# Attention values with tokens on partitions, turned by VectorE, in a fused attention and feed-forward kernel

## The chip, the cores and the metric

The kernel runs on one core of one Trainium2 chip. The metric is the device time of one execution in microseconds (us), as a median over several executions. A profile of one execution lies beside the times. Its engines are PE (TensorE's matmuls), PEld (TensorE's loads of the stationary operand), DVE (VectorE), ACT (ScalarE), POOL (GpSimd) and SP (the engine that issues the DMAs).

## The reference, cut to what matters

Chunked attention with eight memory tokens, then two dense layers with a gate between them, all in float32:

```python
B, H, S, D = 4, 8, 768, 64           # chunk, left_ctx, right_ctx, n_mem = 32, 16, 8, 8
for c in range(S // 32):
    k_full = concat([mem_k, k[:, :, c0 - 16 : c0 + 40]])        # 64 keys per chunk of 32 queries
    v_full = concat([mem_v, v[:, :, c0 - 16 : c0 + 40]])
    scores = (q_c @ k_full.T) / 8
    a = exp(scores - max); a = a / (sum(a) + 1e-9)
    out[:, :, c0 : c0 + 32] = a @ v_full
x = out.transpose(0, 2, 1, 3).reshape(3072, 512)
h = x @ w_in                                                    # 512 -> 2048
g = where(h >= 1, h, where(h <= -1, 0, (h + 1) ** 2 / 4))
return g @ w_out                                                # 2048 -> 512
```

## The kernel before, in words

The 3072 tokens are cut into six blocks of 512. Attention is done for half a block (256 tokens, eight chunks, four pairs of heads) at a time. The dense layers take one block in 16 steps; step s computes 128 of the 2048 hidden columns.

Float32 products of the dense layers are made from three terms: each operand is split into a high part (rounded to the type fp32r) and a low part (the rest), and high by high, low by high and high by low are added up. So x, the attention's output, is kept as `xth` and `xtl`, the gated hidden values as `gh` and `gl`, and the weights as two halves of one tile `wr`. Each x tile has the features of a pair of heads on its 128 partitions and the tokens along its free axis.

Attention of one half block goes through these stages:

- `pe_scores`: 64 small matmuls write scores into a pair of PSUM banks (`ps_s`, tag "s"). The loaded operand is 32 queries wide, the moving one 64 keys, the contraction is the 64 features of a head. The inner loop runs over the two heads, which lie in the two halves of the input partitions.
- `less_max`, an Exp on ScalarE and `normalise`: the softmax, in the tile `pr` with 32 queries of four chunks on the partitions.
- `transpose_prob`: six VectorE transposes of 32 by 32 squares, `pr` to `pt`. Two take all 128 partitions and four take 32 partitions each, since they change the partition group.
- `pe_values`: 64 small matmuls write into the same pair of banks (`ps_x`, tag "s" too). The loaded operand is the values `v` of one head, 64 features wide, and the moving one is `pt`, 32 queries; the output has features on 64 partitions. The half `a` of the input partitions is in the outer loop and the head `h`, which chooses the output partitions, in the inner one.
- `x_high` (ScalarE, two casts out of PSUM into `xth`) and `x_low` (VectorE, two subtractions into `xtl`).

Order is written out by hand, and every engine executes its own instructions in that order. The list `FIRST` orders everything up to the end of the second block: a name such as `n2` stands for the next stage of a half block (n0 to n3 are the halves of the second and third block), `J15` or `E9` for the next stage of a step of the first or second block, `w7` for a part of a weight's decoding, `+` for the next DMA of a list. From the third block on a loop over s sets the order. A step of it issues on TensorE the small matmuls that are due, then `pe_hidden(s)` (12 matmuls of 512 columns into `ps_h`), then `pe_out(s - 2)` (12 into `ps_o`). The gate's instructions for step s - 1 (`gate_sum`, `gate_high`, `gate_low`: writes `gw`, `gh`, `gl`) stand early in step s, and its three ScalarE activations for step s (`gating`) late. Half blocks of the next block begin at steps 3 and 9 (`STARTS`), with scores, softmax, transposes and values one step apart each.

Buffers: `ps_h` has two, `gh` and `gl` three, `gw` and `gt` two, `pr`, `pt`, `qk`, `v` and the "s" banks one, `xth` and `xtl` two.

Of the kernel before, what the change touches and what calls it, by code (L numbers as in the profile page):

```python
# [8 lines left out]
F32 = mybir.dt.float32  # L9
# [33 lines left out]
    w15 J13 J15 n1 J15 n1 J14 C0 J15 n1 J14 n1 n1 C0 n1 n1 J15 C1 n1 n1 J15 n1 C1 n1 n1 C1 C0 C1 C2  # L43
    J15 J15 C0 C1 n1 J15 J15 C0 C2 C2 C0 + n1 C2 n1 n1 C3 C2 C1 C3 C3 D0 C3 C3 C2 D0 D0 D1 D0 D0 n2
    D1 D1 D2 D1 + n2 C3 D1 D2 n2 D0 D2 n2 D2 D3 n2 D2 D1 n2 n2 D3 n2 E4 D3 n2 D3 n2 n2 n2 D2 E4 D3
    n2 E5 n2 E4 E4 E4 D3 E5 E6 E5 E5 E5 E4 E6 E6 E6 n2 E6 E7 + n2 n2 n2 n3 E7 E5 + n3 n3 E7 E8 n3 E7
    n3 n3 n3 E6 n3 E8 n3 n3 n3 E9 n3 n3 n3 E8 n3 E7 E8 E9 E8 E7 + n3 E9 E9 n3 n3 E9 E10 E8 E10 E10
    E10 E11 E10 E9 E11 E11 E11 E12 E11 E10 E12 E12 E12 E13 E12 E11 E13 E13 E13 E14 E13 E12 E14 E14
    E14 E15 E14 E13 E15 E15 E15 E15
"""  # L50

LAST = 2
# [16 lines left out]
def attn_ffn_kernel(ctx: ExitStack, tc: tile.TileContext, first_qk, first_v, qk, vw, w, out):  # L69
# [98 lines left out]
        yield  # L168


    scores_of, prob, prob_t, banks, xts, both = {}, {}, {}, {}, {}, {}

    def x_of(blk):
        if blk not in xts:
# [139 lines left out]
    def transpose_prob(key):  # L314


        src = prob.pop(key).rearrange("p g (s k) -> p g s k", s=2)
        pt = prob_t[key] = apool.tile([P, 2, G, CHUNK], F32, name="pt")
        for b in range(2):
            dve.transpose(pt[:, b], src[:, :, 0])  # L320
            yield
        for b in range(2):
            for a in range(2):
                of, to = (2 * a + b) * CHUNK, (2 * a + 1 - b) * CHUNK
                dve.transpose(pt[to : to + CHUNK, b], src[of : of + CHUNK, :, 1])
                yield

    def pe_values(key):

        ps = banks[key] = two_banks("s", "ps_x")  # L330
        o = ps.rearrange("p a (r t b q) -> p a r t b q", r=NP, t=2, q=CHUNK)
        pt = prob_t.pop(key).rearrange("p b (h r t) q -> p b h r t q", h=2, r=NP)
        v = v_of.pop(key).rearrange("p r (t b h d) -> p r t b h d", t=2, b=2, h=2)
        for r in range(NP):
            for t in range(2):
                for b in range(2):
                    for a in range(2):
                        rows = slice(a * D, (a + 1) * D)
                        for h in range(2):
                            pe.matmul(  # L340
                                o[h * D : (h + 1) * D, a, r, t, b],
                                v[rows, r, t, b, h],
                                pt[rows, b, h, r, t],
                                start=True,
                                stop=True,
                            )
# [10 lines left out]
    def x_high(key):  # L357
        for a in range(2):
            src, hi, _ = x_views(key, a)
            act.copy(hi, src)  # L360

    def x_low(key):
        for a in range(2):
            src, hi, lo = x_views(key, a)
            dve.tensor_tensor(lo, src, hi.bitcast(F32), op=ALU.subtract)
            yield
        banks.pop(key)

    def attention(key):

        pe_scores(key)
        yield
        yield from less_max(key)
        act.activation(prob[key], prob[key], AF.Exp, scale=SCALE)
        yield
        yield from normalise(prob[key])
        yield from transpose_prob(key)
        pe_values(key)
        yield
        x_high(key)  # L380
        yield
        yield from x_low(key)

    def run(*chains):

        chains = [c for c in chains if c is not None]
        while chains:
            chains = [c for c in chains if next(c, chains) is not chains]
# [26 lines left out]
    def gating(s):  # L415

        h = hidden.pop(s)
        g = gpool.tile([P, TB], F32, name="gw", tag="gw")
        t = gpool.tile([P, TB], F32, name="gt")
        act.activation(g, h, AF.Relu, bias=0.5, scale=0.5)  # L420
        act.activation(t, h, AF.Relu, bias=-1.0)
        act.activation(g, g, AF.Square)
        gate[s] = (g, t)
# [6 lines left out]
    def gate_high(s):  # L430
        gh = gpool.tile([P, TB], F32R, name="gh", bufs=3)
        gl = gpool.tile([P, TB], F32R, name="gl", bufs=3)
        act.copy(gh, gate[s])
        gs[s] = (gh, gl)

    def gate_low(s):
        gh, gl = gs[s]
        dve.tensor_tensor(gl, gate.pop(s), gh.bitcast(F32), op=ALU.subtract)
        yield
# [121 lines left out]


    begin = {}
    first = 2
    for blk in range(first + 1, NB):
        for half in range(2):
            begin[(blk - 1) * NFC + STARTS[half]] = (blk, half)
# [4 lines left out]

    steps = NB * NFC
    for s in range(first * NFC, steps):
        k_scores, k_probs, k_trans, k_values = (begin.get(s - stage) for stage in range(4))
        if k_scores is not None:
            pe_scores(k_scores)
            if after(k_scores)[0] < NB:
                load_qk(*after(k_scores))
        if k_values is not None:  # L580
            pe_values(k_values)
            x_high(k_values)
            if after(k_values)[0] < NB:
                load_v(*after(k_values))
        if s > first * NFC:
            gate_sum(s - 1)
            gate_high(s - 1)
        run(
            gate_low(s - 1) if s > first * NFC else None,
            x_low(k_values) if k_values is not None else None,  # L590
        )
        run(
            less_max(k_scores) if k_scores is not None else None,
            normalise(prob[k_probs]) if k_probs is not None else None,
            transpose_prob(k_trans) if k_trans is not None else None,
        )
        if k_scores is not None:
            act.activation(prob[k_scores], prob[k_scores], AF.Exp, scale=SCALE)
        pe_hidden(s)
        gating(s)  # L600
        if s - LAG >= first * NFC:
            pe_out(s - LAG)
            if (s - LAG) % NFC == NFC - 1:
                store((s - LAG) // NFC)
        else:
            n, i = LAST // LAG, s - first * NFC
            for name in items[len(items) - LAST :][i * n : (i + 1) * n]:
                for _ in chains[name]:
                    pass
# [19 lines left out]
def _lay_out(q, k, v, mem_k, mem_v, moe_w_in, moe_w_out):  # L629
    import numpy as _np  # L630

    B, H, S, D = q.shape
    NM, NC = mem_k.shape[2], S // CHUNK
    NP, W = H // 2, NM + LEFT + CHUNK + RIGHT
    NB = B * S // TB

    def windows(mem, a):

        pad = _np.pad(a, ((0, 0), (0, 0), (LEFT, RIGHT), (0, 0)))
        win = [  # L640
            _np.concatenate([mem, pad[:, :, c * CHUNK : (c + 1) * CHUNK + LEFT + RIGHT]], axis=2)
            for c in range(NC)
        ]
        return _np.stack(win, axis=1).reshape(B * NC, H, W, D)

    def transposed(a):

        return a.transpose(1, 3, 0, 2).reshape(NP, 2 * D, -1)


    qt = transposed(q).reshape(NP, 2 * D, NB * 2, TB // 2).transpose(2, 1, 0, 3)
    kw = windows(mem_k, k).reshape(NB * 2, NCH // 4, 2, NP, 2, 2, W // 2, D)

    k0 = kw.transpose(0, 4, 7, 3, 1, 2, 5, 6).reshape(NB * 2, 2 * D, NP, NCH // 2 * W)
    kw = _np.stack([kw[:, :, 0], kw[:, :, 1][..., ::-1, :, :]], axis=2)
    kw = kw.transpose(0, 4, 7, 3, 1, 2, 5, 6).reshape(NB * 2, 2 * D, NP, NCH // 2 * W)
    qk0 = _np.concatenate([qt, k0], axis=3)[0:2].reshape(2, 2 * D, 2, -1).transpose(0, 2, 1, 3)
    qk = _np.concatenate([qt, kw], axis=3).reshape(NB, 2, 2 * D, -1)[1:]
    vw = windows(mem_v, v).reshape(NB, NT, 4, NP, 2, W, D)

    v0 = vw[0].reshape(2, 2, 4, NP // 2, 2, 2, W, D).transpose(0, 3, 1, 6, 4, 2, 5, 7)

    v1 = vw[1:].reshape(NB - 1, 2, NT // 2, 2, 2, NP, 2, W, D).transpose(0, 1, 3, 7, 5, 2, 4, 6, 8)
    DM, DF = moe_w_in.shape
    n = DF // 128

    slices = (
        moe_w_in.reshape(DM // 128, 128, n, 128).transpose(2, 1, 0, 3).reshape(n, 128, DM),
        moe_w_out.reshape(n, 128, DM),
    )  # L670
    w = _np.stack([slices[which][fc] for which, fc in weight_order(n)])
    w = w.reshape(n, 2, 128, DM).transpose(0, 2, 1, 3).reshape(n, 128, 2 * DM)
    arrays = {

        "first_qk": qk0.reshape(NP, 2 * D, -1),
        "first_v": v0.reshape(NP, 2 * W, NCH * D),
        "qk": qk,
        "vw": v1.reshape(NB - 1, 2, 2 * W, -1),
        "w": _np.ascontiguousarray(w).view(_np.int64),
    }  # L680
    return {name: _np.ascontiguousarray(a) for name, a in arrays.items()}
# [23 lines left out]
```

## Time and profile before

| what | value |
|---|---|
| time, median of 3 executions | 599.85 us (599.82 to 600.06) |
| the profiled execution | 600.11 us, of which the span of its instructions is 598.3 us |
| granted TensorE clock | 0.999 |
| busy share of the span: PE, PEld, DVE, ACT | 97%, 81%, 54%, 47% |
| small matmuls of the scores, records | 1536, of 239 ns mean |
| small matmuls of the values, records | 1536, of 226 ns mean |
| DMA | 55.31 MB, mean 92 GB/s |

A row of the table of groups reads: line, engine, operation, what it writes and reads, the shape, the count, then the busy time in us and the mean ns of one instruction, then the idle time of its engine just before. Every instruction of this kernel has line 63, since a helper class records them all, so the rows are told apart by tile names and shapes. Small matmuls of float32 have two records each in the trace: 64 matmuls of a half block give 128 records, and as many loads. In a timeline, a row is a start in us, a duration, an engine and what ran, with `x` and a count where several alike are put together. The chain of waits is the work that ended last, followed back from the end of the span.

### The profile page before, as it was taken

What the parts mean: (1) busy time and instruction counts of PE and PEld (TensorE: products, weight loads), DVE (VectorE), ACT (ScalarE), POOL (GpSimd) and SP (SyncE); (2) the same over time, 40 slices, a digit from 0 to 9 for tenths busy, and PEclk for the clock granted to TensorE, in tenths of its full rate; (3) what the DMA queues carried; (4) which work ended last, traced back from release to release, by engine and by line L of the source; (5) the groups of instructions that cost most, each with busy time, mean ns of one, the idle gap of its engine ahead of it and who ended that gap; (6) DMA issues with size and microseconds to landing.
All of it is one profiled execution on the core that took longest, in us unless ns stands there. A gap on an engine that the chain in (4) does not pass through costs nothing.

```text
span 598.3 us, 12265 instructions
## 1 busy us (share of the span) xinstructions
PE 582.7 (97%) x5496; PEld 483.5 (81%) x5496; DVE 325.6 (54%) x466; ACT 280.3 (47%) x503; POOL 0.7 (0%) x6
## 2 busy tenths in 40 slices
PE   5899999999999999999999999999999999999996
PEld 2888888788888888888888888888888888888885
DVE  5999999986474224636423644623564632322222
ACT  2689864554435335444435443434443444543442
POOL 0000000000000000000000000000000000000000
PEclk9999999999999999999999999999999999999999
DMA  8999300424051004012101223200310000100001
GB/s 355 422 418 419 148 1 0 178 82 168 1 177 71 0 1 158 26 65 108 71 1 71 107 71 107 71 1 34 144 71 2 1 2 0 71 0 1 0 1 70
DMA packets 9844, 55.31 MB, mean 92 GB/s; under 512 B 1088, under 2 KB 1088, under 8 KB 5184
## 3 DMA queue, kind: packets, MB, share of 16 engines
q1 hardware_dynamic: 9792, 54.53, 23.6%
q8 instruction: 43, 0.70, 0.5%
q14 instruction: 9, 0.07, 0.0%
HBM read 48.23 MB, written 6.29 MB: 91 GB/s over the span
## 4 chain that ended last, share of the span: by engine, by line
PE 82%; DVE 15%; issue 2%; DMA 1%; ACT 0%; DVEq 0%; ACTq 0%
PE ps_o L63 38%; PE ps_h L63 38%; DVE f L63 6%; PE ps_x L63 3%; DVE wr L63 2%; PE ps_s L63 2%; DVE gw L63 1%; DVE gl L63 1%; DVE pr L63 1%; DVE den L63 1%; DMA qk<-in_first_qk_dram 1%; DVE pt L63 1%; DVE mx L63 1%; DVE xtl L63 0%; DVE rin L63 0%
## 5 line engine op out<-in xcount | busy, mean ns | idle before, releaser
L63 PE MATMUL ps_h<-xth,wr 128*128 128x512 f32 (+1 forms) x832 | 195.6, 377 | 1.1 <-DVE wr L63 1.1
L63 PE MATMUL ps_o<-wr,gh 128*128 128x512 f32 x768 | 194.7, 390 | 0.0
L63 PEld LDWEIGHTS ps_h<-xth,wr 128*128 128x128 f32 x832 | 149.0, 190 | 30.3 <-DVE wr L63 1.5
L63 PEld LDWEIGHTS ps_o<-wr,gh 128*128 128x128 f32 x768 | 143.3, 188 | 29.4
L63 DVE SCALAR_TENSOR_TENSOR gw<-gw,gt 128x512 f32<-128x512 f32 (+1 forms) x104 | 67.2, 649 | 164.9 <-ACT gw L63 164.6
L63 ACT ACTIVATE gw<-ps_h 128x512 f32<-128x512 f32 (+1 forms) x104 | 58.6, 563 | 159.0 <-PE ps_h L63 158.9
L63 PE MATMUL ps_o<-wr,gl 128*128 128x512 f32 x384 | 106.9, 389 | 0.0
L63 PE MATMUL ps_h<-xtl,wr 128*128 128x512 f32 (+1 forms) x416 | 104.8, 374 | 0.0
L63 DVE TENSOR_TENSOR gl<-gw,gh 128x512 fp32r<-128x512 f32 (+1 forms) x104 | 67.4, 649 | 65.8 <-ACT gh L63 65.7
L63 ACT CAST gh<-gw 128x512 fp32r<-128x512 f32 (+1 forms) x104 | 61.1, 590 | 69.9 <-DVE gw L63 69.9
L63 PEld LDWEIGHTS ps_h<-xtl,wr 128*128 128x128 f32 x416 | 75.3, 190 | 13.9
L63 PEld LDWEIGHTS ps_o<-wr,gl 128*128 128x128 f32 x384 | 72.1, 188 | 15.1
L63 ACT ACTIVATE gw<-gw 128x512 f32<-128x512 f32 (+1 forms) x104 | 62.4, 600 | 0.0
L63 ACT ACTIVATE gt<-ps_h 128x512 f32<-128x512 f32 (+1 forms) x104 | 58.3, 561 | 0.0
L63 DVE STREAM_TRANSPOSE pt<-pr 32x512 f32<-32x512 f32 (+1 forms) x60 | 41.2, 698 | 1.3
L63 DVE SCALAR_TENSOR_TENSOR f<-w,f 128x1024 uint32<-128x1024 uint32 x32 | 39.0, 1220 | 0.4
L63 ACT ACTIVATE pr<-pr 128x1024 f32<-128x1024 f32 (+1 forms) x14 | 13.1, 937 | 35.1 <-DVE pr L63 35.0
L63 PEld LDWEIGHTS ps_x<-pt,v 64*64 64x64 f32 x1536 | 25.1, 142 | 5.0 <-issue 3.3
L63 PE MATMUL ps_x<-pt,v 64*64 64x32 f32 x1536 | 26.6, 226 | 1.2 <-ACT pt L63 1.2
L63 ACT CAST xth<-ps_x 128x512 fp32r<-128x512 f32 x24 | 13.1, 591 | 20.6 <-PE ps_x L63 20.6
L63 ACT CAST wr<-f 128x1024 fp32r<-128x1024 f32 x16 | 16.8, 1051 | 11.7 <-DVE f L63 11.7
L63 PEld LDWEIGHTS ps_s<-qk 64*32 64x32 f32 x1536 | 17.1, 112 | 6.1 <-issue 3.1
(27 smaller groups left out, 182.6 us busy)
## 6 DMA issues: line engine op xcount, KB each, us to landing
w<-in_w_dram SPq DMA_DIRECT2D x16, 1024.0 KB, 19.8
qk<-in_qk_dram SPq DMA_DIRECT2D x10, 1536.0 KB, 6.5
v<-in_vw_dram SPq DMA_DIRECT2D x10, 1024.0 KB, 5.5
out_dram<-ob SPq DMA_DIRECT2D x24, 256.0 KB, 2.0
qk<-in_first_qk_dram SPq DMA_DIRECT2D x4, 768.0 KB, 8.7
v<-in_first_v_dram SPq DMA_DIRECT2D x4, 512.0 KB, 12.7
```

The source lines that it names most:

```text
L63: return self.tc.keep_in_program_order(getattr(self.engine, name)(*args, **kwargs))
```

## The change

From the third block on, `pe_rows` takes the place of `pe_values`. The operands change places: `pt` is loaded, 32 queries wide, and the values `v` move, 64 features. The output has 32 queries on 32 partitions and features along the free axis. `rows_out` copies the two banks to a tile `xr` in SBUF (two ScalarE copies), `turn_rows` transposes its 32 by 32 squares into `xt` with six VectorE instructions, and `split_high` and `split_low` make `xth` and `xtl` out of `xt`, one instruction each over all 1024 columns. `xr` takes the one buffer of `pt` (tag "pt") and `xt` the one of `pr` (tag "pr"). In the loop the values' stage now ends with `split_low` one step later. `FIRST` has a new order in its last four rows. Outside the chip's program, the second half of each window's values is laid out with its 64 features rolled by 32. The first two blocks (n0, n1 and the first attention) stay as they were.

```diff
-    n2 E5 n2 E4 E4 E4 D3 E5 E6 E5 E5 E5 E4 E6 E6 E6 n2 E6 E7 + n2 n2 n2 n3 E7 E5 + n3 n3 E7 E8 n3 E7
...
+    n2 E5 n2 E4 E4 E4 D3 E5 E6 E5 E5 E5 E4 E6 E6 E6 n2 E6 E7 + n2 n2 n2 E7 n3 E5 + n2 n2 E7 E8 E7 n2
...
+    def pe_rows(key, outs):
+        banks[key] = outs
+        pt = prob_t.pop(key).rearrange("p b (h r t) q -> p b h r t q", h=2, r=NP)
+        v = v_of.pop(key).rearrange("p r (t b h d) -> p r t b h d", t=2, b=2, h=2)
+        for r in range(NP):
+            for t in range(2):
+                for b in range(2):
+                    for a in range(2):
+                        rows = slice(a * D, (a + 1) * D)
+                        for h in range(2):
+                            to, c0 = (2 * h + b) * CHUNK, (r * 2 + t) * D
+                            pe.matmul(
+                                outs[a][to : to + CHUNK, c0 : c0 + D],
+                                pt[rows, b, h, r, t],
+                                v[rows, r, t, b, h],
+                                start=True,
+                                stop=True,
+                            )
+    def rows_out(key):
+        xr = rows_of[key] = apool.tile([P, NP, 2, 2, D], F32, name="xr", tag="pt")
+        for a, src in enumerate(banks.pop(key)):
+            act.copy(xr[:, :, :, a], src.rearrange("p (r t d) -> p r t d", r=NP, t=2))
+    def turn_rows(key):
+        src = rows_of.pop(key).rearrange("p r t a (s q) -> p r (t a) s q", s=2)
+        xt = turned[key] = apool.tile([P, NP, HT], F32, name="xt", tag="pr")
+        dst = xt.rearrange("p r (n b q) -> p r n b q", b=2, q=CHUNK)
+        for b in range(2):
+            dve.transpose(dst[:, :, :, b], src[:, :, :, 0])
+            yield
+        for b in range(2):
+            for h in range(2):
+                of, to = (2 * h + b) * CHUNK, (2 * h + 1 - b) * CHUNK
+                dve.transpose(dst[to : to + CHUNK, :, :, b], src[of : of + CHUNK, :, :, 1])
+                yield
+    def split_high(key):
+        act.copy(x_half(x_of(key[0])[0], key[1]), turned[key])
+    def split_low(key):
+        hi, lo = (x_half(x, key[1]) for x in x_of(key[0]))
+        dve.tensor_tensor(lo, turned.pop(key), hi.bitcast(F32), op=ALU.subtract)
+        yield
...
         if k_values is not None:
-            pe_values(k_values)
-            x_high(k_values)
+            ps = two_banks("s", "ps_x")
+            pe_rows(k_values, [ps[:, a] for a in range(2)])
...
             gate_sum(s - 1)
             gate_high(s - 1)
+        if k_values is not None:
+            rows_out(k_values)
         run(
+            split_low(k_split) if k_split is not None else None,
             gate_low(s - 1) if s > first * NFC else None,
-            x_low(k_values) if k_values is not None else None,
         )
...
+            turn_rows(k_values) if k_values is not None else None,
...
         gating(s)
+        if k_values is not None:
+            split_high(k_values)
```

TensorE's order, near the end of `FIRST`, where the second half of the third block (n3) has its values' matmuls. `wr` and a number is a pair of weights, in the order of the steps; `xth` and `xtl` are here those of the second block up to `wr_1316`. Before:

```order
L63 MATMUL ps_h<-xth,wr_984 128x512 x8
L63 MATMUL ps_h<-xtl,wr_984 128x512 x4
L63 MATMUL ps_x<-pt,v 64x32 x64
L63 MATMUL ps_o<-wr_984,gh 128x512 x8
L63 MATMUL ps_o<-wr_984,gl 128x512 x4
```

And with the change:

```order
L63 MATMUL ps_o<-wr_1049,gh 128x512 x8
L63 MATMUL ps_o<-wr_1049,gl 128x512 x4
L63 MATMUL ps_x<-v,pt 32x64 x64
L63 MATMUL ps_h<-xth,wr_1109 128x512 x8
L63 MATMUL ps_h<-xtl,wr_1109 128x512 x4
L63 MATMUL ps_o<-wr_1109,gh 128x512 x8
L63 MATMUL ps_o<-wr_1109,gl 128x512 x4
L63 MATMUL ps_h<-xth,wr_1221 128x512 x8
L63 MATMUL ps_h<-xtl,wr_1221 128x512 x4
```

The values' matmuls of n3 have moved from the middle of the step of `wr_984` to just ahead of the step of `wr_1109`, three steps later, with `wr_944`, `wr_1053` and `wr_1049` now ahead of them; the steps of `wr_1221` and `wr_1316` follow, and then the first step of the third block, which is the first to read n3's x. All other places of small matmuls on TensorE are those of before.

VectorE's order in the loop, in a step with values and the one after it (second half of the fifth block, names with buffer numbers). Before:

```order
L63 STREAM_TRANSPOSE pt_4027<-pr_3946 32x512 x4
L63 SCALAR_TENSOR_TENSOR gw_4047<-gw_4047,gt_4048 128x512
L63 TENSOR_TENSOR gl_4135<-gw_4047,gh_4134 128x512
L63 TENSOR_TENSOR xtl_3761<-ps_x_4064,xth_3760 128x4x2x64 x2
L63 SCALAR_TENSOR_TENSOR gw_4153<-gw_4153,gt_4154 128x512
L63 TENSOR_TENSOR gl_4172<-gw_4153,gh_4171 128x512
```

And with the change:

```order
L63 STREAM_TRANSPOSE pt_4067<-pr_3986 32x512 x4
L63 SCALAR_TENSOR_TENSOR gw_4087<-gw_4087,gt_4088 128x512
L63 TENSOR_TENSOR gl_4173<-gw_4087,gh_4172 128x512
L63 STREAM_TRANSPOSE xt_4179<-xr_4175 128x16x32 x2
L63 STREAM_TRANSPOSE xt_4179<-xr_4175 32x16x32 x4
L63 SCALAR_TENSOR_TENSOR gw_4199<-gw_4199,gt_4200 128x512
L63 TENSOR_TENSOR xtl_3828<-xt_4179,xth_3827 128x4x256
L63 TENSOR_TENSOR gl_4219<-gw_4199,gh_4218 128x512
```

Six transposes stand now between the gate's `gl` of one step and `gw` of the next, and the one subtraction that makes `xtl` ahead of that next step's `gl`.

ScalarE's order at the same kind of place (first half of the fifth block before, and with the change). Before:

```order
L63 ACTIVATE gw_3678<-gw_3678 128x512
L63 CAST xth_3760<-ps_x_3695 128x4x2x64 x2
L63 CAST gh_3767<-gw_3678 128x512
L63 ACTIVATE gw_3786<-ps_h_3773 128x512
L63 ACTIVATE gt_3787<-ps_h_3773 128x512
L63 ACTIVATE gw_3786<-gw_3786 128x512
L63 CAST gh_3804<-gw_3786 128x512
```

And with the change:

```order
L63 ACTIVATE gw_3710<-gw_3710 128x512
L63 CAST gh_3795<-gw_3710 128x512
L63 COPY xr_3798<-ps_x_3727 128x8x64 x2
L63 ACTIVATE gw_3822<-ps_h_3809 128x512
L63 ACTIVATE gt_3823<-ps_h_3809 128x512
L63 ACTIVATE gw_3822<-gw_3822 128x512
L63 CAST xth_3827<-xt_3802 128x4x256
L63 CAST gh_3843<-gw_3822 128x512
```

The cast that makes `gh` has moved ahead of the reads of `ps_x`, and the cast that makes `xth` stands behind the next step's three activations.

More of the change, by code (lines that the diff above doesn't have):

```diff
@@ L45 @@
     D1 D1 D2 D1 + n2 C3 D1 D2 n2 D0 D2 n2 D2 D3 n2 D2 D1 n2 n2 D3 n2 E4 D3 n2 D3 n2 n2 n2 D2 E4 D3
-    n2 E5 n2 E4 E4 E4 D3 E5 E6 E5 E5 E5 E4 E6 E6 E6 n2 E6 E7 + n2 n2 n2 n3 E7 E5 + n3 n3 E7 E8 n3 E7
-    n3 n3 n3 E6 n3 E8 n3 n3 n3 E9 n3 n3 n3 E8 n3 E7 E8 E9 E8 E7 + n3 E9 E9 n3 n3 E9 E10 E8 E10 E10
-    E10 E11 E10 E9 E11 E11 E11 E12 E11 E10 E12 E12 E12 E13 E12 E11 E13 E13 E13 E14 E13 E12 E14 E14
-    E14 E15 E14 E13 E15 E15 E15 E15
+    n2 E5 n2 E4 E4 E4 D3 E5 E6 E5 E5 E5 E4 E6 E6 E6 n2 E6 E7 + n2 n2 n2 E7 n3 E5 + n2 n2 E7 E8 E7 n2
+    E7 n2 E6 n2 E8 n2 n3 E8 E9 E8 n3 E8 E7 n3 E9 n3 E9 n3 n3 n3 E10 E9 E9 E8 E10 n3 n3 E10 n3 E11
+    E10 E10 n3 E9 E11 n3 n3 E11 E12 E11 E11 E10 n3 + E12 n3 E12 n3 n3 E13 E12 E12 n3 E11 E13 n3 n3
+    E13 E14 E13 E13 n3 E12 n3 E14 n3 E14 E15 E14 E14 E13 E15 E15 E15 E15
 """
@@ L168, in decode @@
         yield
-    scores_of, prob, prob_t, banks, xts, both = {}, {}, {}, {}, {}, {}
+    scores_of, prob, prob_t, banks, rows_of, turned, xts, both = {}, {}, {}, {}, {}, {}, {}, {}
+    first = 2
     def x_of(blk):
@@ L367, in x_low, with x_half @@
         banks.pop(key)
+    def pe_rows(key, outs):
[20 more added lines that the diff above has]
+            act.copy(xr[:, :, :, a], src.rearrange("p (r t d) -> p r t d", r=NP, t=2))
+    def x_half(x, half):
+        return x[:, :, half * HT : (half + 1) * HT]
+    def turn_rows(key):
[16 more added lines that the diff above has]
+        yield
     def attention(key):
@@ L377, in attention @@
         yield from transpose_prob(key)
-        pe_values(key)
+        if key[0] < first:
+            pe_values(key)
+            yield
+            x_high(key)
+            yield
+            yield from x_low(key)
+            return
+        ps = two_banks("s", "ps_x")
+        pe_rows(key, [ps[:, a] for a in range(2)])
         yield
-        x_high(key)
+        rows_out(key)
         yield
-        yield from x_low(key)
+        yield from turn_rows(key)
+        split_high(key)
+        yield
+        yield from split_low(key)
     def run(*chains):
@@ L563, in attn_ffn_kernel @@
     begin = {}
-    first = 2
     for blk in range(first + 1, NB):
@@ L574, in attn_ffn_kernel @@
     for s in range(first * NFC, steps):
-        k_scores, k_probs, k_trans, k_values = (begin.get(s - stage) for stage in range(4))
+        k_scores, k_probs, k_trans, k_values, k_split = (begin.get(s - stage) for stage in range(5))
         if k_scores is not None:
@@ L580, in attn_ffn_kernel @@
         if k_values is not None:
-            pe_values(k_values)
-            x_high(k_values)
+            ps = two_banks("s", "ps_x")
+            pe_rows(k_values, [ps[:, a] for a in range(2)])
             if after(k_values)[0] < NB:
@@ L661, in _lay_out @@
     v0 = vw[0].reshape(2, 2, 4, NP // 2, 2, 2, W, D).transpose(0, 3, 1, 6, 4, 2, 5, 7)
-    v1 = vw[1:].reshape(NB - 1, 2, NT // 2, 2, 2, NP, 2, W, D).transpose(0, 1, 3, 7, 5, 2, 4, 6, 8)
+    v1 = vw[1:].reshape(NB - 1, 2, NT // 2, 2, 2, NP, 2, W, D).transpose(0, 1, 3, 7, 5, 2, 4, 6, 8).copy()
+    v1[1:, :, :, :, :, :, 1] = _np.roll(v1[1:, :, :, :, :, :, 1], D // 2, axis=-1)
     DM, DF = moe_w_in.shape
```

## Prediction

> **What bounds the kernel now.** I read the page's busy shares and slices first, then the chain of waits, then the chain in order of time over two steps of the loop, then the groups by shape, and last the timelines of the places that the change touches.
>
> ```profile
> PE 582.7 (97%) x5496; PEld 483.5 (81%) x5496; DVE 325.6 (54%) x466; ACT 280.3 (47%) x503; POOL 0.7 (0%) x6
> ...
> PE   5899999999999999999999999999999999999996
> ...
> DVE  5999999986474224636423644623564632322222
> ...
> PEclk9999999999999999999999999999999999999999
> ...
> PE 82%; DVE 15%; issue 2%; DMA 1%; ACT 0%; DVEq 0%; ACTq 0%
> ```
>
> Each digit is a fortieth of the span, 15 us. VectorE is full up to about 120 us and between 20% and 70% busy after that; TensorE is full throughout at full clock. The chain is TensorE's but for 15% of VectorE, which belong to the early part. The first of the eight half blocks that the change touches has its values here:
>
> ```profile
> 161.64 2.07 PE L63 MATMUL ps_x<-pt,v 64*64 64x32 f32 x128
> ```
>
> So for all eight the price of a thing is what it adds to TensorE's queue. The chain in order of time shows that queue:
>
> ```profile
> 230.39 2.72 PE ps_o L63 x12
> 233.11 1.41 PE ps_s L63 x91
> 234.52 2.97 PE ps_h L63 x12
> 237.49 2.72 PE ps_o L63 x12
> 240.21 2.72 PE ps_h L63 x12
> 242.93 2.72 PE ps_o L63 x12
> 245.65 2.72 PE ps_h L63 x12
> 248.37 2.72 PE ps_o L63 x12
> 251.09 2.00 PE ps_x L63 x128
> 253.09 2.95 PE ps_h L63 x12
> 256.03 2.04 PE ps_o L63 x9
> ```
>
> A plain step lasts from 237.49 to 242.93, 5.44 us. The one with the scores (from 230.39 to 237.49) lasts 7.10, the one with the values (248.37 to 256.03) 7.66. So the values cost 2.22 us of TensorE's time and the scores 1.66, and no piece of another engine lies between: the queue runs without a gap. Each is 64 matmuls of a 64-row contraction.
>
> **The change, part by part.**
>
> *TensorE.* The values' matmuls keep their number and get the scores' shape: 32 columns loaded, 64 moved, where it was 64 loaded and 32 moved.
>
> ```profile
> L63 PE MATMUL ps_x<-pt,v 64*64 64x32 f32 x1536 | 26.6, 226 | 1.2 <-ACT pt L63 1.2
> L63 PEld LDWEIGHTS ps_x<-pt,v 64*64 64x64 f32 x1536 | 25.1, 142 | 5.0 <-issue 3.3 <-ACT pt L63 1.4
> L63 PE MATMUL ps_s<-qk 64*32 64x64 f32 x1536 | 19.6, 239 | 1.1 <-DMA qk<-in_first_qk_dram 1.1
> L63 PEld LDWEIGHTS ps_s<-qk 64*32 64x32 f32 x1536 | 17.1, 112 | 6.1 <-issue 3.1 <-DMA qk<-in_first_qk_dram 2.7
> ...
> 233.03 1.32 PEld L63 LDWEIGHTS ps_s<-qk 64*32 64x32 f32 x128 [0.35 <-issue]
> ...
> 251.01 1.96 PEld L63 LDWEIGHTS ps_x<-pt,v 64*64 64x64 f32 x128 [0.35 <-issue]
> ```
>
> The first four rows are groups over the span, the last two one half block each. A load of 32 columns takes 112 ns and one of 64 takes 142, and 128 of them pass in 1.32 us and 1.96 us: 10 and 15 ns each, so about ten are in flight. The time goes with the columns loaded and not with those moved, which are twice as many in the faster stage. Two things differ between the stages: the shape, which the change takes over from the scores, and the order. The scores change the half of the input partitions with every matmul; `pe_values` and `pe_rows` alike put two matmuls of one half after one another. In the new shape eight matmuls in a row go to eight different places (two halves of the input partitions, four groups of 32 output partitions), as with the scores; before, it was four.
>
> No row shows the new shape in the new order. The nearest from below is the scores' stage at 1.66 us, from above the values' stage at 2.22. I take 1.66, for the shape, the number of places in flight and the two PSUM banks (one for each half of the inputs) are all the scores', and since the old order already kept ten loads in flight. Saved: 7.66 less 7.10 is 0.56 us for each half block, and eight of them (two each in blocks three to six) make 4.5 us.
>
> *VectorE and ScalarE.*
>
> ```profile
> L63 DVE STREAM_TRANSPOSE pt<-pr 32x512 f32<-32x512 f32 x40 | 28.1, 703 | 1.2
> L63 DVE TENSOR_TENSOR wr<-f,wr 128x1024 fp32r<-128x1024 f32 x16 | 19.5, 1218 | 0.0
> L63 ACT CAST wr<-f 128x1024 fp32r<-128x1024 f32 x16 | 16.8, 1051 | 11.7 <-DVE f L63 11.7
> L63 DVE TENSOR_TENSOR xtl<-ps_x,xth 128x512 fp32r<-128x512 f32 x24 | 15.6, 684 | 3.0 <-ACT xth L63 3.0
> L63 ACT CAST xth<-ps_x 128x512 fp32r<-128x512 f32 x24 | 13.1, 591 | 20.6 <-PE ps_x L63 20.6
> L63 ACT COPY ob<-ps_o 128x512 f32<-128x512 f32 x8 | 4.7, 587 | 7.8 <-DVE ob L63 7.8
> ```
>
> Added for a half block on VectorE: six transposes of 0.70, 4.2 us, and one subtraction of 1.22 for two of 0.68, so 4.1 us net, 33 us over the kernel. On ScalarE: two copies of 0.59 take the place of two casts of 0.59, and a cast of 1.05 is new, 8.4 us in all. None of it is on the path as long as the gate keeps up. What it has to keep up with is read from the step with the values:
>
> ```profile
> 251.03 0.69 DVE L63 SCALAR_TENSOR_TENSOR gw<-gw,gt 128x512 f32<-128x512 f32 x1
> 253.15 1.07 ACT L63 CAST xth<-ps_x 128x512 fp32r<-128x512 f32 x2 [3.15 <-PE ps_x L63]
> 254.11 0.63 ACT L63 CAST gh<-gw 128x512 fp32r<-128x512 f32 x1
> 254.78 0.69 DVE L63 TENSOR_TENSOR gl<-gw,gh 128x512 fp32r<-128x512 f32 x1 [3.05 <-ACT gh L63]
> 255.38 1.28 DVE L63 TENSOR_TENSOR xtl<-ps_x,xth 128x512 fp32r<-128x512 f32 x2
> 256.07 0.60 ACT L63 ACTIVATE gw<-ps_h 128x512 f32<-128x512 f32 x1 [1.33 <-PE ps_h L63]
> 257.04 0.63 ACT L63 ACTIVATE gw<-gw 128x512 f32<-128x512 f32 x1
> 257.71 0.69 DVE L63 SCALAR_TENSOR_TENSOR gw<-gw,gt 128x512 f32<-128x512 f32 x1 [1.04 <-ACT gw L63]
> ```
>
> Before, `gh` waited behind the reads of `ps_x` on ScalarE (254.11) and `gl` for it (254.78). Now `gh` goes first: it can start when `gw` is done at 251.7. The values' matmuls end at about 252.5, the two copies to `xr` at about 253.7, and the six transposes at 257.9. Queued behind them is the `gw` of this step, whose inputs are there at 257.1 with the matmuls 0.6 us earlier: it is 0.8 us late and ends at 258.6. ScalarE's cast to `xth` waits for the transposes too and ends at 259.0; behind it stands `gh` (to 259.6), and on VectorE `xtl` (to 260.2) and `gl` (to 260.9). TensorE reads that `gl` two steps on: `ps_o` of this step would stand after three more `ps_h` and two `ps_o`, its first product at about 252.5 + 2.95 + 4 x 2.72, or 266. So about 5 us are left, and a transpose could take 0.70 + 5/6, or 1.5 us, before TensorE waited. The two buffers of `ps_h` are freed by ScalarE's reads at 256.6, which stand ahead of the new cast. Next step's reads wait behind that cast and `gh`, until 259.6, but their matmuls end only at 260.8. So this step's additions cost nothing; the cover is VectorE's and ScalarE's idle time in this step and the next.
>
> The "s" banks are freed by a ScalarE copy (253.7) and no longer by the subtraction (256.7); the scores that reuse them come three steps later at the earliest. `xr` and `xt` take buffers whose last readers (the values' matmuls, the transposes of `pr`) are over by then, and the next write to `pr` is two steps behind `xtl`. On SP, the DMA for `v` still follows the values' matmuls, with the same bytes, and is needed some 30 us later; the queue's order is the same. Nothing is added there.
>
> *The third block's second half,* whose values move three steps later on TensorE, must have its x by the first step of the third block:
>
> ```profile
> 200.31 1.98 PE L63 MATMUL ps_h<-xth,wr 128*128 128x512 f32 x8
> ...
> 216.62 1.98 PE L63 MATMUL ps_h<-xth,wr 128*128 128x512 f32 x8
> ```
>
> The first row is the step that now follows its values, the second the first reader of its x: 16.3 us. Needed are copies 1.2, transposes 4.2, four gate instructions that stand between them 2.8, cast 1.05 and subtraction 1.22, in all 10.5 us; about 6 remain. Cost: nothing.
>
> **Sum.** 4.5 us less. The profiled execution took 600.11 us (598.3 of span), 0.26 above the median; it would take 595.6, with a span of 593.8, and the median 599.85 becomes 595.35.
>
> **Rivals.**
>
> *Same: the order of the matmuls, not the width of the load, sets the pace.* Two matmuls of one half in a row are common to old and new; if these made the difference between 15 and 10 ns for a load, the stage stays at 2.22 us and the time at 599.85. Against it: the load alone is 30 ns longer for 64 columns. For it: no row separates the two.
>
> *Partly:* the order costs about half of what the width gives, a stage near 1.94 and 0.28 saved, 597.6 us. It decides where fewer than the eight places are in flight.
>
> *Slower: two neighbours on one half block each other.* If the second matmul's load can't go on while the first streams its 64 columns, neighbours lose their overlap and the stage takes twice the scores' bare 1.41 us, 2.82 instead of 2.00: 0.82 more for each half block, 606.4 us. It decides from the point where a pair takes over 1.4 times the scores' pair. The Trainium skill has such a rule ("TensorE: Matmul & The Clock Gate", Part 3, "The mechanism"): a load overlaps matmuls in flight only where its row group is another. Against it speak the rows above: the old values had the same neighbours and still passed a load every 15 ns, a tenth of what one takes.
>
> *Faster still: the load's width alone counts.* Half the columns, half of 2.00 us: 1.00 less for each half block, 591.9 us. The scores have just these loads and take 1.41, which speaks against it. "TensorEngine Tiling (Array Packing)", "Performance Considerations", in the Trainium skill advises the swap when the moving side is 32 wide and credits it with four instead of two column tiles; taken at its word that is this case.
>
> *VectorE becomes late* is no case of its own unless a transpose with strided output takes over 1.5 us; I leave it 2% beside the slower one.
>
> **How the numbers follow.** Full saving 75%, in its own range of 594.8 to 596.0 (the bare pieces of the chain differ by 2.00 less 1.41, or 0.59, which gives 4.7 us; executions differ by 0.2); partly 9%; same 6%; slower 7%, of it 2% VectorE; faster still 3%. A change under 0.2%, 1.2 us, can't be told from none. So faster 0.87, same 0.06, slower 0.07. The range leaves out slower, same and nearly all of faster still, and holds the first two cases: 594.2 to 598.7.
>
> **What would show it.** The matmuls `ps_x` by eights of 64 columns: the stage at 1.41 us in the chain, the step at 7.10, the loads at about 112 ns. If the order counts, the loads have 112 ns but the stage is near 2.0. VectorE's busy time should be some 33 us more with no new wait of TensorE; a wait of `ps_o` for `gl` or of `ps_h` for `xtl` after 160 us would prove the cover wrong. Then the transposes of `xt` are the row to look at. The forecast is wrong above all if `ps_x` takes 2 us or more.

## The result and the profile after

The changed kernel takes 595.30 us (median of 4 executions, 595.13 to 595.43), the kernel before, on the same chip, 599.92 us (4 executions, 599.82 to 600.06). The ratio is 0.9923, with a 95% interval of 0.9905 to 0.994. The profiled execution took 595.43 us, with a span of 593.7 us. The page of the changed kernel, busy shares and slices:

```profile
PE 577.6 (97%) x5496; PEld 478.1 (81%) x5496; DVE 357.6 (60%) x506; ACT 288.9 (49%) x511; POOL 0.7 (0%) x6
...
DVE  5999999986576434756723674833584752322222
...
PEclk8599999999999999999999999999999999999999
...
PE 81%; DVE 15%; issue 2%; DMA 1%; ACT 0%; DVEq 0%; ACTq 0%
```

VectorE is busy 32.0 us more than before, ScalarE 8.6 more, TensorE 5.1 less, and the chain has nearly the same shares. The chain in order of time, over the same two kinds of step:

```profile
229.23 2.72 PE ps_o L63 x12
231.95 1.41 PE ps_s L63 x91
233.36 2.97 PE ps_h L63 x12
236.33 2.72 PE ps_o L63 x12
...
247.21 2.72 PE ps_o L63 x12
249.93 1.42 PE ps_x L63 x91
251.34 2.95 PE ps_h L63 x12
254.29 2.72 PE ps_o L63 x12
```

The values now cost what the scores cost: 1.42 us beside 1.41. The step with them lasts from 247.21 to 254.29, 7.08 us; before it was 7.66. That is 0.58 us for each of the eight half blocks, 4.64 in all, and the medians differ by 4.62. Set side by side, the two traces show TensorE 0.58 us further ahead after each of the eight stages. The groups by shape:

```profile
L63 PE MATMUL ps_x<-v,pt 64*32 64x64 f32 x1024 | 11.9, 225 | 0.0
...
L63 PEld LDWEIGHTS ps_x<-v,pt 64*32 64x32 f32 x1024 | 10.6, 105 | 2.8 <-issue 2.8
L63 DVE STREAM_TRANSPOSE xt<-xr 128x512 f32<-128x512 f32 x16 | 10.5, 692 | 8.2 <-ACT xr L63 8.2
...
L63 DVE TENSOR_TENSOR xtl<-xt,xth 128x1024 fp32r<-128x1024 f32 x8 | 9.8, 1226 | 4.6 <-ACT xth L63 4.6
...
L63 ACT CAST xth<-xt 128x1024 fp32r<-128x1024 f32 x8 | 8.4, 1054 | 7.8 <-DVE xt L63 7.8
```

A load of 32 columns takes 105 ns (before, with 64, it was 142 over the span and 135, the median, from 180 us on), the added transposes 0.69 us. Below, a stage is measured from the start of its first small matmul to that of its last, taken from the records of the trace. So measured, the values' stage is 1849 ns before and 1269 after, the scores' stage 1267, the same in each of the eight places.

### The profile page after: what moved, and what is told of

It is laid out like the page before. It is cut to its first block, busy times and chain, and to the rows that moved or that the text cites. A ratio compares the mean times of both kernels' runs of the same rounds, so it can differ in the third digit from the quotient of the medians.

```text
span 593.7 us, 12316 instructions
## 1 busy us (share of the span) xinstructions
PE 577.6 (97%) x5496; PEld 478.1 (81%) x5496; DVE 357.6 (60%) x506; ACT 288.9 (49%) x511; POOL 0.7 (0%) x6
## 4 chain that ended last, share of the span: by engine, by line
PE 81%; DVE 15%; issue 2%; DMA 1%; ACT 0%; DVEq 0%; ACTq 0%
PE ps_o L63 39%; PE ps_h L63 38%; DVE f L63 6%; DVE wr L63 2%; PE ps_s L63 2%; PE ps_x L63 2%; DVE gw L63 1%; DVE gl L63 1%; DVE pr L63 1%; DVE den L63 1%; DMA qk<-in_first_qk_dram 1%; DVE pt L63 1%; DVE mx L63 1%; DVE xtl L63 0%; DVE rin L63 0%
## 5 line engine op out<-in xcount | busy, mean ns | idle before, releaser
L63 PEld LDWEIGHTS ps_o<-wr,gl 128*128 128x128 f32 x384 | 72.1, 188 | 15.1
L63 DVE STREAM_TRANSPOSE xt<-xr 32x512 f32<-32x512 f32 (+1 forms) x48 | 32.9, 699 | 8.8 <-ACT xr L63 8.2
L63 ACT ACTIVATE pr<-pr 128x1024 f32<-128x1024 f32 (+1 forms) x14 | 13.1, 937 | 33.2 <-DVE pr L63 33.0
L63 DVE COPY ob<-ps_o 128x512 f32<-128x512 f32 (+1 forms) x16 | 9.6, 620 | 18.8 <-PE ps_o L63 18.8
L63 PE MATMUL ps_s<-qk 64*32 64x64 f32 x1536 | 19.4, 236 | 1.2 <-DMA qk<-in_first_qk_dram 1.2
```

Source lines behind the costliest of these rows:

```text
L63: return self.tc.keep_in_program_order(getattr(self.engine, name)(*args, **kwargs))
```

## The experiments

Two questions were open: what sets the pace of the small matmuls, and how much work the cover would still have taken. For the first there were two theories. A: the pace comes from the places on the array that are in flight and the columns moved at each. B: it comes from the width of the load alone. The first four experiments and *the kernel before, half of its moved columns* have one execution each; their stages are read from its trace.

**Four matmuls of one half in a row.** The rivals *same*, *partly* and *slower* all rest on neighbours that read one half of the input partitions.

```diff
-                for b in range(2):
-                    for a in range(2):
+                for a in range(2):
+                    for b in range(2):
```

> Four matmuls of one half of the input partitions stand in a row, then four of the other; the eight places of eight matmuls stay the same. My theory (places in flight or loads set the pace, neighbours don't matter): the stage of the values stays at 1.41 us and the time at 595.3. Rival (neighbours on one half block each other): the stage goes from 1.41 towards 2 us or more, which is 0.6 us for each of eight half blocks, 600 us or more.

Measured: 595.44 us, a stage of 1267 ns. The chain in order of time:

```profile
249.89 1.41 PE ps_x L63 x89
```

With four neighbours of one half in place of two, nothing changes. Four neighbours on one half hinder each other no more than two, where four of the other half follow.

**Four places, twice, before the other four.** With `t` inside `b`, the same four places are written twice before the other four have their turn.

```diff
-            for t in range(2):
-                for b in range(2):
+            for b in range(2):
+                for t in range(2):
```

> The same 64 matmuls with the same shapes, in an order in which four places come twice before the other four come, so that four and not eight places are in flight. Theory A (each place loads 32 columns and streams 64 one after the other, and the number of places sets the pace): the records of a place then take 67 to 79 ns each and 32 of them follow one another, so the stage takes 2.1 to 2.5 us in place of 1.41, and the time is 601 to 604. Theory B (each half of the array takes the loads one after another, and their width sets the pace): the stage stays at 1.41 us, the time at 595.3.

Measured: 596.12 us, a stage of 1355 ns, in the chain:

```profile
249.98 1.50 PE ps_x L63 x104
```

Four places in place of eight cost 0.09 us a stage. A's forecast falls, B's is nearly met.

**One half after the other.** The loop over `a` goes outermost: 32 matmuls of one half, then 32 of the other.

```diff
-        for r in range(NP):
-            for t in range(2):
-                for b in range(2):
-                    for a in range(2):
+        for a in range(2):
+            for r in range(NP):
+                for t in range(2):
+                    for b in range(2):
```

> All 32 matmuls of one half of the input partitions come first, then the 32 of the other. The two halves no longer work at the same time. Theory A: four places in flight, a stage of 2.1 to 2.5 us, 601 to 604 us. Theory B: one half's loads alone, twice the stage, 2.7 us, 605.7 us. If the halves did not work in parallel in the changed kernel, nothing changes: 595.3.

Measured: 598.68 us, a stage of 1670 ns, in the chain:

```profile
250.81 1.82 PE ps_x L63 x123
```

Both theories missed. One half alone passes 128 loads in 1670 ns, one in 13; both together one in 10. So two halves are faster than one, but far from twice as fast. The 0.40 us are not all due to the halves: here only four places have their turn at a time, as in the second experiment, which took 1355 ns with both halves. Beside that one, the halves account for about 0.31. What limits one half at 13 ns was not tried further and stays open.

**Half of the moved columns.** Each matmul moves 32 of the 64 features; the rest is left out of the output, and the copies take the computed half twice.

```diff
-                                outs[a][to : to + CHUNK, c0 : c0 + D],
+                                outs[a][to : to + CHUNK, c0 : c0 + D // 2],
...
-                                v[rows, r, t, b, h],
+                                v[rows, r, t, b, h, 0 : D // 2],
```

> Each of the values' matmuls from the third block on moves only the first 32 of the 64 features; the copy out of the banks takes these twice, so the output holds half of what it should. The loads and the places stay. Theory A (load and stream of a place add up): the stage falls well under 1.41 us, to about 0.8, and the time to about 591. Theory B (the loads set the pace): the stage stays at 1.41 us and the time at 595.3.

Measured: 593.96 us, a stage of 1097 ns, in the chain:

```profile
249.60 1.22 PE ps_x L63 x74
```

Halving what is moved saves 0.17 us a stage, and 1.34 us in all: not nothing, as in B, and the stage does not fall to the 0.8 us of A.

**The kernel before, half of its moved columns.** From the third block on, `pe_values` of the kernel before moves 16 of 32 queries; the other queries are left out of the output, and the casts and subtractions are cut into pieces that use the computed ones twice.

```diff
+                            q = CHUNK if key[0] < 2 else CHUNK // 2
...
-                                o[h * D : (h + 1) * D, a, r, t, b],
-                                pt[rows, b, h, r, t],
+                                o[h * D : (h + 1) * D, a, r, t, b, 0:q],
+                                pt[rows, b, h, r, t, 0:q],
```

> The kernel before, but from the third block on each of the values' matmuls moves only 16 of the 32 queries (loaded are 64 features as before); the casts and subtractions take the 16 twice, in twice as many smaller instructions, so the output holds half of what it should. Theory (the width of the load sets the pace in the old shape too): the stage of the values stays within 0.2 us of 2.00, the time within 1.5 us of 599.9. Rival (the moved columns count as much as the loaded): the 64 matmuls get a quarter shorter or more, 1.6 us or less for the stage, 596.7 us or less.

Measured: 600.48 us, beside 600.19 us for the kernel before (median of 12 executions); the stage is 1849 ns, as with all 32. The chain and two groups:

```profile
251.25 1.99 PE ps_x L63 x128
```

```profile
L63 PEld LDWEIGHTS ps_x<-pt,v 64*64 64x64 f32 x1536 | 25.3, 142 | 5.5 <-issue 3.5 <-ACT pt L63 1.7
L63 PE MATMUL ps_x<-pt,v 64*64 64x16 f32 x1024 | 16.4, 207 | 0.0
```

In the old shape halving the moved columns changes nothing: a record of a matmul is 13 ns shorter from 180 us on (206 ns for 219, medians), and the stage is the same. With 64 columns loaded, what sets the pace is not what is moved. In the new shape, loading 32, it counts a little. So A holds in neither shape, and B fits the old one alone.

**The change in the loop alone.** `FIRST` and the third block's two half blocks stay as before; the six half blocks of blocks four to six are changed.

```diff
-    n2 E5 n2 E4 E4 E4 D3 E5 E6 E5 E5 E5 E4 E6 E6 E6 n2 E6 E7 + n2 n2 n2 E7 n3 E5 + n2 n2 E7 E8 E7 n2
+    n2 E5 n2 E4 E4 E4 D3 E5 E6 E5 E5 E5 E4 E6 E6 E6 n2 E6 E7 + n2 n2 n2 n3 E7 E5 + n3 n3 E7 E8 n3 E7
...
-        if key[0] < first:
+        if key[0] <= first:
```

> The change is done in the loop alone (six half blocks of blocks four to six); the third block's two and the hand-written order are those of before. Theory (each changed stage saves 0.56 to 0.59 us and nothing else counts): six times that, 3.4 to 3.5 us under before, 596.4 to 596.5 us. Rival (the new order by hand brings part of the gain): clearly nearer to 599.9 or to 595.3 than that.

Measured: 596.40 us (596.22 to 596.61), the kernel before, run beside it, 600.15 us, ratio 0.9939 (0.9924 to 0.9953). It is 3.75 us faster; six times 0.58 is 3.5, eight times 4.64. Most of the 0.27 over lies ahead of the change: its first changed stage starts 0.17 us earlier than in the trace before (250.85 for 251.02), behind work that is alike in both, and from there to the end it takes 3.5 us less. So the gain goes by half blocks, and the new order in `FIRST` shows no cost or gain of its own.

**No transposes.** The six transposes are left out, and x goes on in the wrong layout.

```diff
-        dst = xt.rearrange("p r (n b q) -> p r n b q", b=2, q=CHUNK)
-        for b in range(2):
-            dve.transpose(dst[:, :, :, b], src[:, :, :, 0])
-            yield
...
+        turned[key] = rows_of.pop(key).rearrange("p r t a d -> p r (t a d)")
```

> The six transposes of a half block are left out (x is then in a wrong layout); copies, cast and subtraction stay. Theory (the transposes lie under TensorE's work and cost nothing): 595.3 us as with them. Rival (VectorE's added 33 us cost some of the gain through contention or late gates): lower than 595.3 by what they cost, at most some us.

Measured: 595.24 us (595.15 to 595.31). VectorE is busy 325.1 us, 32.5 less, and the time is that of the changed kernel. The transposes cost nothing.

**Every transpose twice, and three times.**

```diff
-            dve.transpose(dst[:, :, :, b], src[:, :, :, 0])
+            for _ in range(2):
+                dve.transpose(dst[:, :, :, b], src[:, :, :, 0])
...
-                dve.transpose(dst[to : to + CHUNK, :, :, b], src[of : of + CHUNK, :, :, 1])
+                for _ in range(2):
+                    dve.transpose(dst[to : to + CHUNK, :, :, b], src[of : of + CHUNK, :, :, 1])
```

> Each of the six transposes is done twice, 4.2 us more VectorE work for a half block. Theory (some 5 us are left before TensorE waits for the gate): still 595.3 us, at most 0.3 more. Rival (the cover is already used up): up to 4.2 us for each of eight half blocks, up to 629 us.

> Each of the six transposes is done three times, 8.4 us more VectorE work for a half block. Theory (about 5 to 7 us are left): the gate's high part of the step with the values comes about 1.8 us too late for its second layer; six half blocks in the loop give 11 us and the two of the third block up to 5 more: 605 to 611 us, with waits of ps_o for gh in the trace. Rival (VectorE has room for it in the whole span, 60% busy, so that it does not matter): 595.3 us.

Measured: twice 595.24 us (595.1 to 595.3), ratio 0.9919 (0.9904 to 0.9933); three times 619.26 us (619.22 to 620.82), ratio 1.0328 (1.031 to 1.0345), both to the kernel before. By VectorE's busy time a half block has 4.2 and 8.5 us more than in the changed kernel. So 4.2 us more are free, and 8.5 cost 24 us in all. The three-times forecast missed by 8 us and more. TensorE's waits after 160 us, three times:

```profile
PE ps_o L63 <- ACT gh L63: 12.4, 7, 2.0
PE ps_h L63 <- ACT gt L63: 1.9, 1, 1.9
PE ps_x L63 <- DVE pt L63: 0.9, 2, 0.4
```

The kernel before, the changed kernel and the one with doubled transposes have none there. The forecast had the first row in mind, the step's own `gh`, and came near to it: set beside the changed kernel's trace, the second layer of each of the six half blocks in the loop starts 2.2 us late, 13.1 in all (forecast 1.8 and 11), and the third block loses 2.9 (forecast up to 5). The third row it had not: the values' matmuls waiting for `pt`. The values' stages of the three second halves in the loop are stretched, to 2836, 1572 and 1610 ns, 2.2 us together. The other 6 us or so lie in the steps that follow a late second layer.

**Fifteen transposes.** This lies between the two: 6.3 us more than the change has.

```diff
+            for _ in range(2):
+                dve.transpose(dst[:, :, :, b], src[:, :, :, 0])
...
+                for _ in range(3 - (b == 1 and h == 1)):
+                    dve.transpose(dst[to : to + CHUNK, :, :, b], src[of : of + CHUNK, :, :, 1])
```

> Fifteen transposes in place of six, 6.3 us more VectorE work for a half block, between the doubled and the tripled ones. By the prediction's about 5 us of room: TensorE waits 1.3 us in each of eight half blocks, 605 us or more. By the trace of the doubled one, where the gate's high part is there 2.3 us before its use: the loop costs nothing and the third block's second half at most 0.8 us, 595.3 to 596.1 us.

Measured: 601.84 us (9 executions, 601.70 to 602.04), ratio to the kernel before 1.0027 (1.0017 to 1.0037), 6.5 us more than the changed kernel. Both forecasts missed, one above and one below. TensorE's waits after 160 us, and the timeline of the step's own gate:

```profile
PE ps_x L63 <- DVE pt L63: 3.1, 8, 0.4
PE ps_h L63 <- ACT gt L63: 0.2, 1, 0.2
```

```profile
252.85 10.82 DVE L63 STREAM_TRANSPOSE xt<-xr 128x512 f32<-128x512 f32 x15 [0.53 <-ACT xr L63]
...
264.66 0.61 ACT L63 CAST gh<-gw 128x512 fp32r<-128x512 f32 x1
...
265.39 0.90 PE L63 MATMUL ps_o<-wr,gh 128*128 128x512 f32 x3
```

The `gh` of the step, which the forecast watched, is ready at 265.27 and read at 265.39: just in time. The cost lies one half block further on. The timeline there, of this kernel, then of the changed kernel, and the maximum in the kernel with doubled transposes:

```profile
271.67 1.22 DVE L63 TENSOR_REDUCE mx<-ps_s 128x16 f32<-128x1024 f32 x1
...
283.62 4.24 DVE L63 STREAM_TRANSPOSE pt<-pr 128x512 f32<-128x512 f32 x6
...
286.26 0.48 PE L63 MATMUL ps_x<-v,pt 64*32 64x64 f32 x8
287.17 0.30 PE L63 MATMUL ps_x<-v,pt 64*32 64x64 f32 x4 [0.43 <-DVE pt L63]
287.91 1.39 PE L63 MATMUL ps_x<-v,pt 64*32 64x64 f32 x116 [0.44 <-DVE pt L63]
```

```profile
269.34 1.22 DVE L63 TENSOR_REDUCE mx<-ps_s 128x16 f32<-128x1024 f32 x1 [0.43 <-PE ps_s L63]
...
281.37 4.24 DVE L63 STREAM_TRANSPOSE pt<-pr 128x512 f32<-128x512 f32 x6
...
285.80 1.48 PE L63 MATMUL ps_x<-v,pt 64*32 64x64 f32 x128
```

```profile
269.09 1.23 DVE L63 TENSOR_REDUCE mx<-ps_s 128x16 f32<-128x1024 f32 x1
```

In the changed kernel `pt` is done at 285.61, and the values' matmuls that read it start at 285.80: 0.19 us of room. The scores of this half start at 268.29 with 15 transposes, at 267.82 in the changed kernel and at 267.57 with doubled ones, so the maximum follows them by 3.38, 1.52 and 1.52 us. The doubled ones' backlog is gone by then; with 15, VectorE is still behind with the gate and the maximum is 1.9 us late. In the three steps up to `pt` next to nothing makes it up: `pt` starts 1.8 us late, again beside the scores. TensorE starts on the first pieces of `pt` and waits for the others. The three second halves' stages in the loop take 2822, 3215 and 3147 ns, 5.4 us more than 3 x 1.27; the third block's second half adds 0.5 (its values come at 197.43, the next half's at 250.22, 52.79 later, where the change has 197.60, 249.86 and 52.26). That is 5.9 of the 6.3 by which the spans differ.

## Why the prediction was right, point by point

*TensorE's queue sets the time.* Right: no wait of TensorE after 160 us, and the saving of the steps is the saving of the kernel, for eight half blocks and for six.

*The values' stage takes the scores' time.* Right: 1269 ns beside 1267, a step of 7.08 us (forecast 7.10), 0.58 us saved (forecast 0.56). Of the three likenesses that the prediction gave as its reason (shape, places in flight, two banks), the shape carries most; the two banks, one for each half, are common to old and new. The stage went from 1.85 us, in the old shape with four places, to 1.36 with the shape alone (four places again, the second experiment) and to 1.27 with eight places. So 0.49 of the 0.58 us are the swap of loaded and moved operand, 0.09 the places; which half comes next counted nothing with two or four matmuls of a half in a row. In the shape it is the narrower load that pays: with 32 columns moved in both, the stage is 1849 ns with 64 loaded and 1097 with 32 (eight places). How the 10 ns per load come about is not shown.

*The rivals.* *Same* and *partly* needed two neighbours of one half to cost time; the result has them and takes the scores' time, and so do four in a row. *Slower* needed such neighbours to block each other; they do not. The rule of the Trainium skill behind it ("TensorE: Matmul & The Clock Gate", Part 3, "The mechanism") says that a load overlaps matmuls in flight only where its row group is another. The first and the third experiment disagree: four in a row of one row group take 1267 ns, and with 32 in a row a load still passes every 13 ns, where one load takes 106. Only the whole stage sorted by half costs something, 0.40 us. *Faster still* held that the width alone counts and halves the 2.00 us. It comes to 1.42, and to 1.22 even with the moved columns kept at 32. The Trainium skill ("TensorEngine Tiling (Array Packing)", "Performance Considerations") credits the swap at 32 moved columns with four column tiles, where 64 loaded columns have two. Here that is a factor of 0.71, and of 0.61 with 32 moved, not the 0.5 that twice the tiles would give.

*VectorE's and ScalarE's additions are free.* Right: with and without the transposes the time is the same within 0.06 us. Their sizes were right too (0.69 us a transpose, 1.05 the cast, 1.23 the subtraction). The timeline of the step with the values, in the changed kernel:

```profile
250.59 0.62 ACT L63 CAST gh<-gw 128x512 fp32r<-128x512 f32 x1 [1.75 <-DVE gw L63]
...
251.38 1.07 ACT L63 COPY xr<-ps_x 128x512 f32<-128x512 f32 x2 [0.17 <-PE ps_x L63]
252.49 4.19 DVE L63 STREAM_TRANSPOSE xt<-xr 128x512 f32<-128x512 f32 x6 [0.55 <-ACT xr L63]
...
256.70 0.69 DVE L63 SCALAR_TENSOR_TENSOR gw<-gw,gt 128x512 f32<-128x512 f32 x1
256.71 1.05 ACT L63 CAST xth<-xt 128x1024 fp32r<-128x1024 f32 x1 [0.78 <-DVE xt L63]
...
257.66 0.62 ACT L63 CAST gh<-gw 128x512 fp32r<-128x512 f32 x1
257.79 1.22 DVE L63 TENSOR_TENSOR xtl<-xt,xth 128x1024 fp32r<-128x1024 f32 x1 [0.39 <-ACT xth L63]
...
258.93 0.68 DVE L63 TENSOR_TENSOR gl<-gw,gh 128x512 fp32r<-128x512 f32 x1
...
265.00 1.30 PE L63 MATMUL ps_o<-wr,gh 128*128 128x512 f32 x5
```

This is the order that the prediction worked out: `gh` first, `gw` behind the transposes, then the cast, `gh`, the subtraction and `gl`. Counted from the start of the values' matmuls (249.86 here, 251.02 before), `gl` ends after 9.75 us (forecast 9.9) and the second layer starts after 15.1 (forecast 15.0).

*"About 5 us are left", 1.5 us for a transpose.* This is the step that failed, though it cost the forecast nothing. The room at this gate is larger, since the second layer's first matmuls read `gh` and not `gl`: `gh` ends at 258.28 and is read at 265.00, 6.7 us (`gl` is read at 266.82). With 6.3 us more work, 6.6 with the gaps between the transposes, it was just in time. But the time is already 6.5 us worse there, for the backlog runs on into the second half block, six steps after the first, whose `pt` had 0.19 us to spare. The limit lies between 4.2 us more (free) and 6.3 (not free). That the 5 falls between them is luck, as it was reckoned for another tile: the prediction looked at the reader of the delayed instruction and not at what stands behind it on VectorE in the next steps.

*The third block's second half.* Right. In the changed kernel:

```profile
197.60 1.49 PE L63 MATMUL ps_x<-v,pt 64*32 64x64 f32 x128
...
208.24 1.23 DVE L63 TENSOR_TENSOR xtl<-xt,xth 128x1024 fp32r<-128x1024 f32 x1 [1.12 <-ACT xth L63]
...
215.46 1.98 PE L63 MATMUL ps_h<-xth,wr 128*128 128x512 f32 x8
```

From the end of the values' matmuls (199.1) to that of `xtl` (209.47) are 10.4 us (forecast 10.5), and the first reader stands at 215.46, 6.0 later (forecast about 6).

No version here that computes the whole output beats the changed kernel beyond the noise. The first two blocks, which still have the old values, were not tried.

## What to carry to other kernels

Where both operands of a small float32 matmul fit either way, load the narrower one: with 64 features and 32 queries that took the stage from 1.85 to 1.27 us, and the order of the matmuls hardly mattered as long as both halves of the input partitions took turns. Work put on an engine that is idle 40% of the time is free only up to a point that no busy share shows: follow the backlog down that engine's queue to the next place that is just in time, not only to the reader of the first instruction that comes late. Doubling or tripling the added work is a quick way to find that point.

## What the runs showed of the hardware that was not expected

Of the two shapes, moved columns count only in the one with the narrow load. With 64 columns loaded, half of the moved ones changed nothing (1849 ns and 1849); with 32 loaded, it took off 172 ns of 1269.

One half of the input partitions passes a load every 13 ns, both together every 10; two halves gave a factor of 1.3 and not 2 (1.2 beside the order with four places, 1355 ns).

A stage of small matmuls lengthens its step by more than its own time, at both of its ends together: 7.08 less 5.44 is 1.64 us for a stage of 1.27 from first to last start. The scores do the same (1.66).

The slice of the page at 15 to 30 us has a granted clock of 0.5 in the changed kernel and 0.9 in the profiled execution before. It is no effect of the change: the kernel before with half of its moved columns, which is the kernel before up to 160 us, shows 0.6 in this slice. Nor did it cost time: the kernel before ran at a mean clock of 0.984 in 600.07 us and at 0.999 in 600.30. VectorE is full in that part.
